# A windowed-attention, gated and mixer kernel: three loads moved ahead by a turn, and dummy matmuls in three waits

## The chip, the core and the metric

The kernel runs on one core of one Trainium2 chip. The metric is the device time of one execution in microseconds, less is better; it is given as the median of several runs. Its engines are TensorE (PE, with its weight loads PEld), VectorE (DVE), ScalarE (ACT), GpSimd (POOL) and SyncE (SP), which issues all of the DMAs here, in one queue.

## The reference

Three blocks follow each other: attention over a window of 64 keys, a gated block whose gate is mixed over the positions by `w_spatial`, and a token and channel mixer. Cut to what matters:

```python
# q, k, v: (4, 8, 576, 64)
scores = 0.125 * q @ k.T                       # only where 0 <= query - key < 64
attn = softmax(scores)
x = (attn @ v)  ->  (4, 576, 512)

h = relu(x @ w_in)                             # w_in: 512 x 1024
u, v = h[..., :512], h[..., 512:]
v_n = (v - mean(v)) / sqrt(var(v) + 1e-6)
v_s = einsum('ts,bsd->btd', w_spatial, v_n) + b_spatial      # w_spatial: 576 x 576
x = (u * v_s) @ w_out                          # w_out: 512 x 512

xt = x.transpose(0, 2, 1)                      # token mixer, then channel mixer
u = x + (relu(xt @ w_tok1) @ w_tok2).transpose(0, 2, 1)
out = u + relu(u @ w_ch1) @ w_ch2
```

The float64 weights are converted on the chip from their integer words; q, k, v and `w_spatial` are float32. Products of float32 accuracy are made of three matmuls, each operand being split into a high part (a cast on ScalarE) and a low part (a subtraction on VectorE).

## The kernel before, in words

The first part of the program (to some 220 us) is attention together with the gated block. Its order is written out by hand for every engine (`tc.manual_schedule`); each engine runs its instructions in that order. Behind it a scheduler orders the rest.

Attention goes over 18 iterations, `its`, each with up to 128 query rows of 8 heads. The loop over `n`, lines 517 to 553, is one *turn* each. Turn `n` does, for TensorE: the transposes of the normalised probabilities `pt(n)` (`att_turn`, line 283), one piece of the queued work (`run_work`), the products with v, `xo(n)` (`att_pv`, line 295), the scores of iteration `n + 2` (`scores`, lines 236 and 241), and then more queued work until a budget is used. ScalarE copies the transposes to SBUF (`PT(n)`, line 284), makes the exponentials of iteration `n + 1` (`sexp`, line 264), then converts `w_in` parts (L72, L441), casts `vf` (L355) and `xh(n)` (L309). VectorE normalises the exponentials (`snorm`, lines 272 to 274), writes `xl(n)` (L310), the maxima of the scores of iteration `n + 2` (`smax`, line 252 in the first iterations, line 255 from iteration 6 on) and other conversions.

The queued work consists of `uv_v` (12 matmuls per iteration: the v half of `x @ w_in`), `uv_u` (the u half, four groups of 12 matmuls every three iterations) and `spatial` (the product with `w_spatial`, from turn 7 on; its sums L392 and L393 run on VectorE and free the PSUM bank). Three PSUM banks (`psmm`) serve this work, four (`psa`, tag `sp`) the scores and transposes, and one (tag `xo`) the products with v. A bank is given to its next user when its last reader is done.

The loads: q and k of an iteration (`load_qk`, two buffers each) and v (`load_v`, two buffers each) are issued two turns ahead of their scores' or products' turn. `w_spatial` comes in ten parts, `ws_parts`; `load_ws(n)` at the end of a turn issues the next `n` parts into `raw` (three buffers) and has them cast to high (L101) and low parts (L103) in the same place of the order. `ws_at` says how many parts a turn takes. ScalarE's casts thus stand ahead of the next turn's copies PT. The first `w_out` loads (lines 569 and 570) use the same three buffers afterwards; they are ordered by the scheduler.

Before the loop, iterations 0 and 1 are scored and `w_in` is converted in parts. `keep_busy(k)` issues `k` matmuls of the identity, whose result nobody reads. Before, six of them stand before `pt(0)` and two before `pt(1)`.

Of the kernel before, what the change touches and what calls it, by code (L numbers as in the profile page):

```python
# [8 lines left out]
F32 = mybir.dt.float32  # L9
# [11 lines left out]
P = 128  # L21
# [14 lines left out]
def tile_kernel(ctx, tc, qT, kT, kE, v, w_in, wsT, b_sp, w_out, w_t1, w_t2, w_c1, w_c2, outT):  # L36

    nc = tc.nc

    def pool(name, side=None, stack=ctx, **kw):  # L40
        return stack.enter_context(tc.tile_pool(name=name, side=side, **kw))
# [4 lines left out]
    ident16 = const.tile([P, P], BF16, name="ident16")  # L46
# [58 lines left out]
    def load_split(*a, **kw):  # L105

        for _ in split_steps(*a, **kw):  # L110
            pass
# [55 lines left out]
    psmm = pool("psmm", bufs=3, space=PSUM)  # L167
# [7 lines left out]
    ws_h = ws[:, :5 * S].rearrange("p (k c) -> p k c", k=5)  # L175
    ws_l = ws[:, 5 * S:10 * S].rearrange("p (k c) -> p k c", k=5)
# [4 lines left out]
    att = pool("att", "right", stack=a_stack, bufs=2)  # L181
    psa = pool("psa", stack=a_stack, bufs=4, space=PSUM)

    def keep_busy(n):

        ps = psmm.tile([P, 512], F32, tag="mm", name="mm")
        for _ in range(n):
            nc.tensor.matmul(ps.rearrange("p (a c) -> p a c", a=4), ident16, ident16.unsqueeze(1).to_broadcast([P, 4, 128]), start=True, stop=True)

    its = [(p, i) for p in range(B // 2) for i in range(9)]  # L190
    held, vheld, soft, xt, vn = {}, {}, {}, {}, {}

    def where(p, i):

        return (2 * p + (i - 1) // 4, (i - 1) % 4) if i else (None, None)

    def load_qk(n):
        p, i = its[n]
        qq = att.tile([P, 4, 128], F32, tag="qq", name="qq")
        nc.sync.dma_start(out=qq.rearrange("p j t -> p (j t)"), in_=qT[n])  # L200
        kk = att.tile([P, 4, 256], F32, tag="kk", name="kk")
        if i:
            nc.sync.dma_start(out=kk.rearrange("p j k -> p (j k)")[:, :768], in_=kT[8 * p + i - 1])
            kk = kk.rearrange("p j k -> p (j k)")[:, :768].rearrange("p (j k) -> p j k", k=192)
        else:
            nc.sync.dma_start(out=kk.rearrange("p j k -> p (j k)"), in_=kE[p])
        held[n] = (qq, kk)

    def load_v(n):
        p, i = its[n]  # L210
        b, m = where(p, i)
        va = att.tile([P, 512], F32, tag="va", name="va")
        vb = att.tile([P, 512], F32, tag="vb", name="vb")
        if i:
            nc.sync.dma_start(out=va, in_=v[b, 128 * m:128 * m + 128, :])
            nc.sync.dma_start(out=vb, in_=v[b, 128 * m + 64:128 * m + 192, :])
        else:
            nc.sync.dma_start(out=va, in_=v[2 * p, S - 64:S + 64, :])
            nc.sync.dma_start(out=vb, in_=v[2 * p + 1, S - 64:S + 64, :])
        vheld[n] = (va, vb)  # L220
# [27 lines left out]
    def smax(n, g):  # L248
        scs, pb, nm, sm, mk = soft[n]
        if mk is None:  # L250
            mx = att.tile([P, 4], F32, tag="mx", name="mx", bufs=3)
            nc.vector.tensor_reduce(out=mx, in_=scs[g], op=ALU.max, axis=AX.X)
        else:
            for h in range(4):
                nc.vector.tensor_tensor_reduce(  # L255
                    out=pb[:, 4 * g + h, :], in0=scs[g][:, h, :], in1=mk, scale=-SCALE, scalar=3e38,
                    op0=ALU.add, op1=ALU.min, accum_out=nm[:, 4 * g + h:4 * g + h + 1])
            return
        nc.vector.tensor_scalar(out=nm[:, 4 * g:4 * g + 4], in0=mx, scalar1=-SCALE, scalar2=None, op0=ALU.mult)
# [13 lines left out]
        nc.vector.reciprocal(out=rs, in_=rs)  # L273
        nc.vector.tensor_tensor(out=pb[:, hs, :], in0=pb[:, hs, :], in1=rs.unsqueeze(2).to_broadcast([P, w, 128]), op=ALU.mult)  # L274

    def att_turn(n, banks=None):
        pb = soft.pop(n)[1]
        PT = att.tile([P, 8, 128], F32, tag="PT", name="PT", bufs=1)
        for g in range(2):
            pt = (banks.tile([P, 512], F32, tag="mm", name="pt").rearrange("p (h k) -> p h k", h=4) if banks  # L280
                  else psa.tile([P, 4, 128], F32, tag="sp", name="pt"))
            for h in range(4):
                nc.tensor.transpose(pt[:, h, :], pb[:, 4 * g + h, :], ident)  # L283
            nc.scalar.copy(out=PT[:, 4 * g:4 * g + 4, :], in_=pt)  # L284
        return PT

    def att_pv(n, PT, now=True):
        p, i = its[n]
        vt = vheld.pop(n)
        xo = psa.tile([P, 4, 128], F32, tag="xo", name="xo", bufs=1)  # L290
        for j in range(4):
            for q in range(2):
                for e in range(2):
                    hc = slice(64 * (2 * j + e), 64 * (2 * j + e) + 64)
                    nc.tensor.matmul(xo[64 * e:64 * e + 64, j, 64 * q:64 * q + 64], vt[q][:, hc],  # L295
                                     PT[:, 4 * e + j, 64 * q:64 * q + 64], start=True, stop=True)
        held[n] = xo
# [46 lines left out]
    def uv_v(p, i):  # L344

        xh, xl = xt[p, i // 3]
        ts_ = slice(128 * (i % 3), 128 * (i % 3) + 128)
        ps = psmm.tile([P, 512], F32, tag="mm", name="mm")
        mm3(ps, [(xh[:, k, ts_], xl[:, k, ts_], wi_h[:, k, 512:], wi_l[:, k, 512:]) for k in range(4)], late=(0, 1, 2) if p + i > 1 else (0, 2, 1))
        vv = lp.tile([P, 512], F32, tag="vf", name="vf", bufs=2)  # L350
        turns.append(normalise(p, i, ps, vv))
        tick()
# [21 lines left out]
    def tick():  # L374
        for t in list(turns):
            if next(t, turns) is turns:
                turns.remove(t)
# [36 lines left out]

    ws_parts = [(k, c) for k in range(5) for c in (0, 288)]

    def load_ws(n):
        for k, c in ws_parts[:n]:
            rows = P if k < 4 else 64
            load_split(ws_h[:, k, c:c + 288], ws_l[:, k, c:c + 288], wsT[128 * k:128 * k + rows, c:c + 288], rows=rows, dup=k == 4)  # L420
        del ws_parts[:n]

    def w_part(raw, src, hi, lo, cols):
# [29 lines left out]
    with tc.manual_schedule(engines={E.PE, E.SP, E.Activation, E.DVE, E.Pool}):  # L453
        wv = [wv_part(k) for k in range(4)]
        wu = [wu_part(ft) for ft in range(4)]

        def go(*ws):
            for w in ws:
                next(w, 0)

        load_qk(0)
        go(wv[0])
        load_qk(1)
        go(wv[1])
        load_v(0)
        go(wv[2])
        go(wv[3])
        go(wv[0])
        scores(0)
        smax(0, 0)  # L470
        smax(0, 1)
        go(wv[0])
        sexp(0, 0)
        go(wv[1])
        sexp(0, 1)
        go(wv[0])
        snorm(0, 0)
        snorm(0, 1)
        load_qk(2)
        load_v(1)  # L480
        go(wu[0])
        scores(1)
        keep_busy(6)
        PT = att_turn(0)
        smax(1, 0)
        smax(1, 1)
        go(wv[0])
        go(wv[1])
        go(wv[2])
        go(wv[1])  # L490
        go(wv[2])
        go(wv[3])
        att_pv(0, PT)
        go(wv[2])
        sexp(1, 0)
        go(wv[1])
        go(wv[3])
        go(wv[3])
        sexp(1, 1)
        go(wv[2])  # L500
        go(wv[3])
        load_v(2)
        load_qk(3)
        go(wu[1])
        go(wu[2])
        load_qk(4)
        go(wu[3])
        load_v(3)
        nc.sync.dma_start(out=bb, in_=bass.AP(b_sp.tensor, b_sp.offset, [[0, P], [1, S]]))
        scores(2)  # L510
        snorm(1)
        smax(2, 0)
        smax(2, 1)
        uv_v(*its[0])
        conv, late = {1: (0,), 2: (1, 2), 3: (3,)}, ()
        ws_at = {3: 2, 4: 3, 5: 3, 6: 2}
        for n in range(1, len(its)):
            more, some = n + 2 < len(its), n + 1 < len(its)
            cv = [wu[i] for i in conv.get(n, ())]
            if more and n > 1:  # L520
                if n > 2:
                    load_qk(n + 2)
                load_v(n + 2)
            if n == 1:
                keep_busy(2)
            PT = att_turn(n)
            go(*late)
            go(*late)
            go(*cv[:1])
            go(*cv[:1])  # L530
            if some:
                sexp(n + 1, 0)
                sexp(n + 1, 1)
                snorm(n + 1)
            go(*cv[:1])
            go(*cv[:1])
            tick()
            left = BUDGET - run_work(1)
            go(*cv[1:])
            att_pv(n, PT)  # L540
            go(*cv[1:])
            if more:
                scores(n + 2)
                smax(n + 2, 0)
                smax(n + 2, 1)
            if n > 1:
                tick()
            late = cv[1:]
            while work and left > 0:
                left -= run_work(1)  # L550
                tick()
            load_ws(ws_at.get(n, 0))
            enable(n)
        while turns:
            tick()
# [486 lines left out]
```

## Time and profile before

| | us |
|---|---|
| median of 3 runs (642.7, 644.18, 645.35) | 644.18 |
| the profiled execution | 642.67 |
| its span in the profile | 640.9 |
| TensorE busy in the span | 612.3 |
| VectorE busy | 461.9 |
| ScalarE busy | 333.4 |

The profile is of one execution. Its timeline gives for each group of instructions the start and the duration, and in brackets the idle time of the engine before it and what ended that; its windows give the busy time of engines in stretches of the span, with the clock that TensorE was granted (1.00 is 2.4 GHz, 0.50 is 1.2 GHz) and the share of time that DMA engines were busy. TensorE is busy for 96% of the span, the idle time lying mostly in the first 80 us, around 175 us and between 280 and 340 us.

### The profile page before, as it was taken

To read this page: it belongs to the slowest core of one execution; us is meant where nothing else is said; L and a number is where in the kernel's file an instruction comes from. 1 tells how busy PE (TensorE), PEld (TensorE's weight loads), DVE (VectorE), ACT (ScalarE), POOL (GpSimd) and SP (SyncE) were. 2 spreads that over 40 slices of the span, in tenths; PEclk is the share of its full clock that TensorE was granted. 3 is DMA by queue.
4 is the path that set the end of the run, shared out by engine and by line. 5 is a ranking of instruction groups with operands and counts; after the bars stand their busy time and mean duration, and the time that the engine had idled before them with its cause. 6 is when DMAs were issued, how large, how long until landed. Compare 5 with 4: busy or idle time off the path is not lost.

```text
span 640.9 us, 11957 instructions
## 1 busy us (share of the span) xinstructions
PE 612.3 (96%) x4440; PEld 570.2 (89%) x4440; DVE 461.9 (72%) x973; ACT 333.4 (52%) x835; POOL 151.9 (24%) x166
## 2 busy tenths in 40 slices
PE   6689799999999999999899999999999999999997
PEld 3468599899879999888798999999999999999987
DVE  4786757755575689678968973188976998867982
ACT  4677663444784264667544443355543646344550
POOL 6600000100000010556452582032000440002510
PEclk9889899999999999999999999999999999999999
DMA  8832653422240034557753719058434576534872
GB/s 324 279 98 97 200 167 96 146 76 75 76 156 27 2 107 145 181 200 237 292 191 118 263 74 337 1 170 281 139 134 132 201 229 211 164 115 139 269 241 75
DMA packets 46105, 103.60 MB, mean 162 GB/s; under 512 B 4192, under 2 KB 16736, under 8 KB 46048
## 3 DMA queue, kind: packets, MB, share of 16 engines
q1 hardware_dynamic: 46048, 102.84, 47.8%
q8 instruction: 35, 0.57, 0.4%
q14 instruction: 22, 0.18, 0.1%
HBM read 83.95 MB, written 18.87 MB: 160 GB/s over the span
## 4 chain that ended last, share of the span: by engine, by line
PE 67%; DVE 13%; ACT 7%; DMA 5%; issue 4%; POOL 2%; SPq 0%; DVEq 0%; ACTq 0%; POOLq 0%
PE mm L161 31%; PE A L894 17%; PE mm L823 7%; PE A L823 5%; ACT pb L264 3%; DMA scr<-hl 2%; PE pt L283 2%; PE xo L295 2%; DMA k<-in_w_c 2%; POOL k L728 1%; PE sc L241 1%; DVE ol L889 1%; DVE k L68 1%; DVE pb L274 1%; DVE k L69 1%
## 5 line engine op out<-in xcount | busy, mean ns | idle before, releaser
L894 PE MATMUL A<-oh,w 128*128 128x384 f32 x480 | 102.7, 334 | 0.0
L876 POOL TENSOR_TENSOR H<-H 128x384 f32<-128x384 f32 x36 | 44.8, 1258 | 182.6 <-DVE ol L889 171.2
L889 DVE TENSOR_TENSOR ol<-H,oh 128x384 fp32r<-128x384 f32 x120 | 79.8, 697 | 10.5 <-ACT oh L888 8.3
L894 PEld LDWEIGHTS A<-oh,w 128*128 128x128 f32 x480 | 85.0, 188 | 0.0
L888 ACT CAST oh<-H 128x384 fp32r<-128x384 f32 x120 | 59.8, 512 | 42.0 <-PE A L894 33.3
L894 PE MATMUL A<-ol,w 128*128 128x384 f32 x240 | 61.2, 336 | 2.2 <-DVE ol L889 2.2
L161 PE MATMUL mm<-ws,nh 128*128 128x288 f32 x320 | 61.9, 297 | 0.0
L161 PEld LDWEIGHTS mm<-ws,nh 128*128 128x128 f32 x320 | 49.9, 188 | 0.5 <-issue 0.3
L361 POOL TENSOR_SCALAR rstd<-mv 128x1 f32<-128x1 f32 x18 | 4.5, 249 | 184.1 <-DVE mv L360 183.9
L894 PEld LDWEIGHTS A<-ol,w 128*128 128x128 f32 x240 | 43.1, 188 | 3.2 <-DVE ol L889 3.1
L876 DVE TENSOR_TENSOR H<-H 128x384 f32<-128x384 f32 x36 | 23.6, 654 | 21.6 <-ACT H L816 19.3
L161 PE MATMUL mm<-ws,nl 128*128 128x288 f32 x128 | 37.7, 295 | 0.0
L264 ACT ACTIVATE pb<-pb,nm 128x128 f32<-128x128 f32 x96 | 37.2, 398 | 0.4 <-DVE nm L255 0.3
L272 DVE TENSOR_SCALAR rs<-sm 128x8 f32<-128x8 f32 (+1 forms) x19 | 3.2, 171 | 47.1 <-ACT pb L264 47.1
L284 ACT COPY PT<-pt 128x512 f32<-128x512 f32 x36 | 19.5, 591 | 30.8 <-PE pt L283 30.8
L161 PE MATMUL mm<-xh,wi_h 128*128 128x384 f32 x96 | 32.7, 341 | 0.7 <-ACT vf L355 0.6
L161 PE MATMUL mm<-xh,wi_l 128*128 128x384 f32 x96 | 32.1, 335 | 0.0
L161 PE MATMUL mm<-xl,wi_h 128*128 128x384 f32 x96 | 32.1, 334 | 0.0
L148 ACT CAST hl<-k 128x512 fp32r<-128x512 f32 (+1 forms) x24 | 13.6, 569 | 31.7 <-DVE k L69 16.3
L161 PE MATMUL mm<-gh,wo_l 128*128 128x512 f32 (+1 forms) x80 | 29.4, 370 | 0.0
L161 PE MATMUL mm<-gl,wo_h 128*128 128x512 f32 (+1 forms) x80 | 29.4, 370 | 0.0
L161 PE MATMUL mm<-gh,wo_h 128*128 128x512 f32 (+1 forms) x80 | 29.3, 376 | 0.0
(180 smaller groups left out, 1709.2 us busy)
## 6 DMA issues: line engine op xcount, KB each, us to landing
w<-scr SPq DMA_DIRECT2D x63, 512.0 KB, 4.3
k<-in_w_c SPq DMA_DIRECT2D x24, 512.0 KB, 5.5
scr<-hl SPq DMA_DIRECT2D x18, 512.0 KB, 5.1
kk<-in_kT SPq DMA_DIRECT2D x16, 384.0 KB, 4.9
k<-sums SPq DMA_DIRECT2D x12, 512.0 KB, 3.2
qq<-in_qT SPq DMA_DIRECT2D x18, 256.0 KB, 4.3
va<-in_v SPq DMA_DIRECT2D x18, 256.0 KB, 2.8
vb<-in_v SPq DMA_DIRECT2D x18, 256.0 KB, 3.1
```

Source lines behind the costliest of these rows:

```text
L68: nc.vector.scalar_tensor_tensor(out=y, in0=high, scalar=-0x80000000, in1=y, op0=ALU.bitwise_and, op1=ALU.bitwise_or)
L148: nc.scalar.copy(out=hi, in_=x)
L161: nc.tensor.matmul(o, a, c, start=(i == 0), stop=(i == n - 1))
L264: nc.scalar.activation(out=pb[:, h, :], in_=scs[g][:, h - 4 * g, :] if mk is None else pb[:, h, :], func=AF.Exp, scale=SCALE if mk is None ...
L283: nc.tensor.transpose(pt[:, h, :], pb[:, 4 * g + h, :], ident)
L284: nc.scalar.copy(out=PT[:, 4 * g:4 * g + 4, :], in_=pt)
L295: nc.tensor.matmul(xo[64 * e:64 * e + 64, j, 64 * q:64 * q + 64], vt[q][:, hc], PT[:, 4 * e + j, 64 * q:64 * q + 64], start=True, stop=True)
L823: nc.tensor.matmul(o, a, m, start=first and i == 0, stop=i == len(todo) - 1, skip_group_check=True)
L876: eng.tensor_tensor(out=out, in0=a, in1=b, op=ALU.subtract)
L888: nc.scalar.copy(out=oh, in_=blk[j])
L889: nc.vector.tensor_tensor(out=ol, in0=blk[j], in1=f(oh), op=ALU.subtract)
L894: nc.tensor.matmul(acc[d], a, m, start=(first and j == 0 and i == 0), stop=(last and j == NJ - 1 and i == 2), skip_group_check=True)
```

## The change

- q and k of iteration `n + 3` are loaded at the start of turn `n`, instead of those of `n + 2`; v stays at `n + 2`.
- `load_ws` first completes the casts of the parts that its last call issued, then issues its own, without casting them. `ws_at` begins one turn earlier (turns 2 to 5 instead of 3 to 6, with the same numbers of parts).
- Seven dummy matmuls, written to the bank `xo`, stand before `uv_v(0)`. The two before `pt(1)` now write to the bank that the transposes use afterwards, and eight such stand before `pt(2)`.

```diff
-    def keep_busy(n):
-
-        ps = psmm.tile([P, 512], F32, tag="mm", name="mm")
+    def keep_busy(n, ps=None):
+
+        ps = ps or psmm.tile([P, 512], F32, tag="mm", name="mm")
...
-    def att_turn(n, banks=None):
+    def att_turn(n, banks=None, busy=0):
...
+            for _ in range(0 if g else busy):
+                nc.tensor.matmul(pt, ident16, ident16.unsqueeze(1).to_broadcast([P, 4, 128]), start=True, stop=True)
...
+    ws_open = []
+
     def load_ws(n):
+
+        for t in ws_open:
+            for _ in t:
+                pass
+        ws_open.clear()
         for k, c in ws_parts[:n]:
             rows = P if k < 4 else 64
-            load_split(ws_h[:, k, c:c + 288], ws_l[:, k, c:c + 288], wsT[128 * k:128 * k + rows, c:c + 288], rows=rows, dup=k == 4)
+            ws_open.append(split_steps(ws_h[:, k, c:c + 288], ws_l[:, k, c:c + 288], wsT[128 * k:128 * k + rows, c:c + 288], rows=rows, dup=k == 4))
+            next(ws_open[-1])
...
+        keep_busy(7, psa.tile([P, 512], F32, tag="xo", name="xo", bufs=1))
         uv_v(*its[0])
...
-        ws_at = {3: 2, 4: 3, 5: 3, 6: 2}
+        ws_at = {2: 2, 3: 2, 4: 3, 5: 3}
...
-            if more and n > 1:
-                if n > 2:
-                    load_qk(n + 2)
-                load_v(n + 2)
-            if n == 1:
-                keep_busy(2)
-            PT = att_turn(n)
+            if n > 1:
+                if n + 3 < len(its):
+                    load_qk(n + 3)
+                if more:
+                    load_v(n + 2)
+            PT = att_turn(n, busy={1: 2, 2: 8}.get(n, 0))
```

How this moves instructions, at three places. SP in turns 4 and 5 (`qq` and `kk` are q and k, `va` and `vb` v, `raw` the buffers of the spatial weights), before:

```order
L215 DMA va<-in_v 128x512
L216 DMA vb<-in_v 128x512
L85 DMA raw<-in_wsT 128x288 x3
L200 DMA qq<-in_qT 128x512
L203 DMA kk<-in_kT 128x768
```

The same place on SP in the changed program, with the end of turn 3 ahead of it:

```order
L85 DMA raw<-in_wsT 128x288 x2
L200 DMA qq<-in_qT 128x512
L203 DMA kk<-in_kT 128x768
L215 DMA va<-in_v 128x512
L216 DMA vb<-in_v 128x512
L85 DMA raw<-in_wsT 128x288 x3
```

The parts that are cast at the end of turn 4 are now the two at the top of this piece; the three at its foot are those that turn 5 casts. In the piece from before, the three `raw` loads are cast in turn 4 itself.

ScalarE from the end of turn 3 into turn 5 (`ws` are the spatial weights, `PT` the copied transposes, `pb` the exponentials), before:

```order
L101 CAST ws<-raw 128x288 x2
L284 COPY PT<-pt 128x512 x2
L264 ACTIVATE pb,sm<-sc,nm 128x128 x8
L355 ACTIVATE vf<-mm 128x512
L309 CAST xh<-xo 128x4x128
L101 CAST ws<-raw 128x288 x3
```

And in the changed program:

```order
L101 CAST ws<-raw 128x288 x2
L286 COPY PT<-pt 128x512 x2
L264 ACTIVATE pb,sm<-sc,nm 128x128 x8
L357 ACTIVATE vf<-mm 128x512
L311 CAST xh<-xo 128x4x128
L101 CAST ws<-raw 128x288 x2
```

The casts stand in the same places; at the end of turn 4 there is one less, and at the end of turn 6, further down, three instead of two.

TensorE between `uv_v(0)` and the transposes of turn 1 (`mm` and `pt` are PSUM banks, `ident` the identity), before:

```order
L161 MATMUL mm<-wi_l,xh 128x512 x4
L188 LDWEIGHTS ident_63
L188 MATMUL mm<-ident_63 128x512
L188 LDWEIGHTS ident_63
L188 MATMUL mm<-ident_63 128x512
L283 MATMUL pt<-ident,pb 128x128 x8
```

And in the changed program:

```order
L161 MATMUL mm<-wi_l,xh 128x512 x4
L283 LDWEIGHTS ident_63
L283 MATMUL pt<-ident_63 128x512
L283 LDWEIGHTS ident_63
L283 MATMUL pt<-ident_63 128x512
L285 MATMUL pt<-ident,pb 128x128 x8
```

The two dummies stay where they were but write to `pt`. The seven stand in front of the first row of `uv_v(0)`, and eight more pairs like these stand in front of the transposes of turn 2. From turn 3 on TensorE's order is the same in both programs.

## Rows read from the trace of the kernel before

**Rows 1.** Windows, one stretch: us, busy time (and count) of each engine, clock, DMA.

```profile
80.00:96.00 16.00, 16.00 (x177) 15.57 (x178) 8.35 (x31) 10.41 (x42) 0.79 (x2) 1.00 0.51 166
```

**Rows 2.** Timeline of TensorE, turns 0 to 2: start, us, line, tile, count, [idle before].

```profile
22.34 0.51 PE L161 MATMUL mm<-wi_h,xh 128*128 128x512 f32 x1 [0.93 <-ACT wi_h L441]
...
25.81 0.91 PE L188 MATMUL mm<-ident 128*128 128x512 bf16 x2
...
26.56 1.04 PE L283 MATMUL pt<-ident,pb 128*128 128x128 f32 x8
...
33.54 1.94 PE L283 MATMUL pt<-ident,pb 128*128 128x128 f32 x8 [2.44 <-DVE pb L274]
```

**Rows 3.** Windows of 1 us, TensorE alone: us, busy time, granted clock, DMA share, GB/s.

```profile
25.00:26.00 1.00, 1.00 (x4) 0.50 1.05 412
...
75.00:76.00 1.00, 1.00 (x6) 0.50 0.92 270
```

**Rows 4.** Timeline of VectorE and ScalarE, turns 0 to 2.

```profile
19.05 0.69 DVE L310 TENSOR_TENSOR xl<-xo,xh 128x512 fp32r<-128x512 f32 x1 [0.36 <-ACT xh L309]
...
24.17 1.22 DVE L274 TENSOR_TENSOR pb<-pb,rs 128x1024 f32<-128x1024 f32 x1
...
27.25 1.07 ACT L284 COPY PT<-pt 128x512 f32<-128x512 f32 x2 [0.61 <-PE pt L283]
...
36.00 0.64 ACT L72 ACTIVATE mm<-U 128x512 f32<-128x512 f32 x1
...
36.57 0.35 ACT L264 ACTIVATE pb<-sc,nm 128x128 f32<-128x128 f32 x1
```

**Rows 5.** Timeline of TensorE, turn 4.

```profile
58.06 1.04 PE L283 MATMUL pt<-ident,pb 128*128 128x128 f32 x8
58.85 1.18 PE L161 MATMUL mm<-wi_h,xh 128*128 128x512 f32 x4
...
61.80 0.34 PE L295 MATMUL xo<-PT,va 128*64 128x64 f32 x4
...
62.88 1.10 PE L241 MATMUL sc<-kk,qq 64*64 64x128 f32 x32
```

**Rows 6.** Timeline of ScalarE and VectorE, end of turn 4 and turn 5.

```profile
63.61 0.66 ACT L309 CAST xh<-xo 128x512 fp32r<-128x512 f32 x1
66.48 0.80 ACT L101 CAST ws<-raw 128x288 fp32r<-128x288 f32 x2 [2.20 <-DMA raw<-in_wsT]
...
68.91 1.06 ACT L284 COPY PT<-pt 128x512 f32<-128x512 f32 x2
69.87 0.41 ACT L264 ACTIVATE pb<-pb,nm 128x128 f32<-128x128 f32 x1
...
66.32 0.28 DVE L255 CUSTOM_DVE_ANT_0 pb<-sc,msk 128x128 f32<-128x128 f32 x1
```

**Rows 7.** Timeline of TensorE, starts of turns 5 and 6, first `uv_u` of turn 6.

```profile
65.16 1.06 PE L283 MATMUL pt<-ident,pb 128*128 128x128 f32 x8 [1.18 <-DVE pb L274]
...
74.90 1.94 PE L283 MATMUL pt<-ident,pb 128*128 128x128 f32 x8 [2.69 <-DVE pb L274]
...
82.07 0.44 PE L161 MATMUL mm<-xh,wi_h 128*128 128x384 f32 x1
```

**Rows 8.** The tile `raw`, 40 to 100 us: time from issue to landing.

```profile
DMA to landing us min/median/max: 2.6/3.3/3.8
```

**Rows 9.** Timeline of VectorE, turn 7: last subtractions, first spatial sum.

```profile
92.04 0.83 DVE L103 TENSOR_TENSOR ws<-raw,ws 128x288 fp32r<-128x288 f32 x2
...
98.08 0.45 DVE L392 TENSOR_TENSOR tmp<-mm,bb 128x288 f32<-128x288 f32 x1
```

**Rows 10.** Chain of the work that ended last: start, us, what.

```profile
3.05 7.55 DMA U<-in_w_in
...
97.36 7.78 PE mm L161 x56
```

**Rows 11.** DMA issues, 40 to 100 us: count, KB each, median us to landing.

```profile
raw<-in_w_out SPq DMA_DIRECT2D x5, 256.0 KB, 3.5
```

## The prediction, made before the change was run

> **What bounds the kernel now.** I read the windows by stretch first. From 80 to 96 us TensorE is busy for the whole window at the full clock [rows 1]; the idle time further down, around 175 us and from 280 us on, lies where the change leaves the order of work as it is, apart from a few loads of `w_out`. What it can win or lose therefore lies in the first 80 us, and whatever it wins there moves all later work forward. In that first part I then read TensorE's timeline together with those of ScalarE and VectorE. Three things cost time.
>
> First, turns 0 to 2. TensorE waits for short chains on ScalarE and VectorE, and after such waits its matmuls run at half speed: nine matmuls of `uv_v(0)` go from 22.34 to 25.81, and the transposes `pt(2)` take 1.94 us after an idle time of 2.44 [rows 2]. The granted clock in 25 to 26 us is 0.50, the 1.2 GHz level [rows 3]. Second, at the end of turn 4 ScalarE stands in front of the casts of the spatial weights (L101) until their loads land, and the copies of the transposes, PT(5), stand behind these casts [rows 6]. Third, that delay reaches TensorE as an idle time of 2.69 us before `pt(6)` at 74.90 [rows 7], and turn 6 starts at the 1.2 GHz level again [rows 3].
>
> **Dummies, part one: seven before `uv_v(0)`, two before `pt(1)`.** The seven write the bank of `xo(0)`, so the first waits until VectorE has read it: xl(0) ends at 19.05 + 0.69 = 19.74 [rows 4]. One matmul of 512 columns takes (61.80 - 58.85) / 12 = 0.25 us at full clock [rows 5], so seven end at 21.5. The first three matmuls of `uv_v(0)` then end at 22.2, before the fourth, which starts at 22.34 and waits for a cast, not for TensorE. So at full clock the dummies cost nothing. They fill most of the idle time between the scores and `uv_v(0)`, and I take it that the clock stays up; then nine matmuls take 9 x 0.25 = 2.2 us and end at 24.55 instead of 25.81. The two dummies behind them only change place and bank; they end at 25.05. `pt(1)` needs the normalised pb(1), written until 24.17 + 1.22 = 25.39 [rows 4]. With 0.15 us for the handover it starts at 25.55 instead of 26.56 [rows 2]: **1.0 us**, no more, since VectorE is next.
>
> **Dummies, part two: eight before `pt(2)`.** PT(1), the exponentials of turn 2 and its normalisation all hang on `pt(1)`, so `pt(2)` moves from 33.54 to 32.5. The scores of turn 3 end where TensorE's 2.44 us of idle time begin, at 33.54 - 2.44 = 31.1, now 30.1. Eight dummies take 2.0 us and end at 32.1, before pb(2) is there: no cost, by 0.4 us. With the clock up, `pt(2)` and its copies take as long as in turn 1, where the copies start 0.69 after the transposes and end 1.76 after them (26.56; 27.25 + 1.07) [rows 2, 4], so PT(2) ends at 34.3. ScalarE then runs L72 and reaches the exponentials 0.57 later (36.00 to 36.57), at 34.85 [rows 4]. VectorE's maxima for them follow the normalisation directly and move with `pt(2)`; before, they were done shortly ahead of the exponentials, now they arrive together with ScalarE. The exponentials move from 36.57 to 34.85, that is **1.7 us** for both parts, of which the second brings 0.7. From there to the first `uv_u` of turn 3 VectorE is occupied almost without a gap, and I carry the 1.7 through it unchanged.
>
> **Loads of the spatial weights a turn ahead.** In turn 4 the casts are now two instead of three, and their data were issued in turn 3. ScalarE ends xh(4) at 63.61 + 0.66 = 64.27; two casts take 0.80, to 65.07 [rows 6]. The copies need the transposes, 65.16 + 0.69 = 65.85 [rows 4, 7]. So PT(5) starts at 65.85 instead of 68.91, and the exponentials of turn 6 at 66.81 instead of 69.87 [rows 6]: **3.1 us**. VectorE writes the maxima from 66.32 on [rows 6], just in time. Then normalisation and `pt(6)` follow at 71.84 instead of 74.90. TensorE is ready before that: `uv_v` ends at about 68.9, the outputs and scores take 2.2 more, 71.1. So VectorE's normalisation is next in line, and 0.7 us of idle time are left where there were 2.69.
>
> Does the clock hold over this 0.7? TensorE had 1.18 idle before `pt(5)` [rows 7] and ran on at full speed. So I take full clock for turn 6: from `pt` to the first `uv_u` it took 82.07 - 74.90 = 7.17 [rows 7]; the same work in turn 4 took 62.88 + 1.10 - 58.06 = 5.92 [rows 5]. That is 1.25, rounded **1.3 us**.
>
> Each load has to arrive. The second load of turn 3 reuses the buffer of a part cast at the end of that turn, so SP waits there; by the ends above it is issued some 5 us before its cast, and these loads land within 3.8 us [rows 8]. In turn 4 two of three loads wait for that turn's subtractions, about 69 us, and land near 72.5; the casts of turn 5 then end near 73 and PT(6) near 74, while TensorE asks for it only at 75.6 after `uv_v`. Covered by 1.5 us. Behind the waiting SP stand q and k of three turns ahead and v of two, none of which is needed within 8 us.
>
> **q and k three turns ahead: nothing.** Before, no matmul in turns 3 to 12 waits for them; they land earlier and compete with loads that have time. It costs up to the 0.5 us that a delayed cast might take out of the 1.5 of cover, so nothing in the sum.
>
> **The sum.** 1.7 + 3.1 + 1.3 = 6.1 us. The profiled execution took 642.67 (span 640.9 and 1.77 around it), which gives 636.6; the median of three is 644.18, 1.51 higher, and I forecast against it: **638.1 us**. The bounds of the parts: dummies from -0.9 (if the clock is down when they start, eight take 512 columns / 1.2 GHz = 0.43 each, 3.4 in all, and push `pt(2)` from 32.5 to 33.5, while seven push `uv_v(0)` behind its cast) to 1.7 and another 1.5, if the runs above the profiled one are long because their clock falls oftener. The loads from 2.2 to 3.1, the clock of turn 6 from 0 to 1.3.
>
> The Trainium skill (TensorE: Matmul & The Clock Gate, Part 1) says that the point at which the clock changes shifts from run to run of one kernel. The three runs here, 2.65 us apart, would agree with that but don't show that it is the clock. By it the clock terms of one profile are one draw of several.
>
> **Rivals.** (a) *The dummies buy nothing.* The clock falls anyway, or VectorE absorbs what turn 1 wins. For it: VectorE is the next bound everywhere in turns 1 to 3. Against: ScalarE waits over 2 us for the slow transposes of `pt(2)`. Then 3.1 + 1.3 remain, 639.8; without the clock of turn 6 also 641.1.
>
> (b) *The casts still wait.* The buffers, three of them, are refilled only after the subtractions, so a load "a turn ahead" may be issued late. If the casts of turn 4 wait as long as the last one did before, only the dummies' 1.7 and some of the rest are left: 641 to 642.5.
>
> (c) *The output weights block VectorE: slower.* The first w_out loads now queue on SP behind the last spatial weights; they wait for the subtractions at 92.04 to 92.9 [rows 9] and their first conversion stands on VectorE before turn 7's spatial sums (L392), which give TensorE its PSUM buffers back. TensorE needs the first at 97.36 + 7.78 / 4 = 99.3 [rows 10], when the first of four groups ends; before, the sum was done at 98.08 + 0.45 [rows 9]. Counting back over normalisation and conversion, the load has to land by about 96.9. Issued at 92.5 with the median landing of 3.5 [rows 11] it is there at 96.0. With the longest wait for a load in this trace, 7.55 [rows 10], it lands at 100.1 and TensorE stops for 3.2: 641.3. Slower than before by over 0.5% only from a landing of some 14 us. The Trainium skill (DMA: Bandwidth & Descriptors, Latency and other measured facts) gives 0.2 us of memory latency on average and 2 us at high load; by it alone the landing would grow by 1.8, a stop of under 1 us and about 639. No run here shows that.
>
> **How the numbers follow.** Faster or slower "by over 0.5%" means 3.2 us, about what a measurement of this kernel can tell from no change. Forecast, 635 to 640: 0.67. Rival (a): 0.18, two thirds of it faster by over 0.5%. Rival (b): 0.08, a quarter of it. Rival (c): 0.07, half of it slower or near, since other late collisions of moved loads belong here too. Faster: 0.64 + 0.12 + 0.02 = 0.78 less 0.02 for the edge at 641, so 0.76; slower 0.04; the rest 0.20. The range takes the forecast's low end and reaches over (a) to the middle of (b): 635.0 to 641.5.
>
> **What would show it.** Right: seven dummies from about 19.7, granted clock 1.00 throughout 23 to 37 us, `pt(2)` near 32.5 and about 1 us long, no ScalarE wait for the spatial weights at the end of turn 4, `pt(6)` at 74.90 - 4.8 = 70.1 and about 1 us long, first `uv_u` of turn 6 at 76.0. Wrong: a half-clock stretch in the first 80 us, casts that still wait in turn 4, or an idle TensorE behind VectorE in turn 7.

## The result, and the profile after

The changed kernel takes 638.37 us (median of 6 runs, 636.93 to 639.03), the kernel before beside it 643.44 (6 runs, 642.13 to 645.35). The ratio is 0.9918, with a 95% interval from 0.9899 to 0.9937: faster by 5.1 us. The forecast was 638.1. It is nearer to the measured time than its sum is to the measured gain: 6.1 us had been taken off a median of 644.18, and more runs of the kernel before put that median 0.74 lower. That two errors of the same sign cancel in the time is luck.

The profiled execution took 636.93 us, its span is 5.7 us shorter. The page of the changed kernel (span; busy time, share and count of TensorE; its granted clock in 40 slices, in tenths):

```profile
span 635.2 us, 11997 instructions
...
PE 610.3 (96%) x4455; PEld 567.5 (89%) x4455; DVE 461.6 (73%) x973; ACT 332.9 (52%) x835; POOL 152.3 (24%) x166
...
PEclk9999999999999999999999999999999999999999
```

TensorE is busy for 2.0 us less, although it runs 15 more dummies: fewer of its matmuls run at half speed. The windows of two stretches (us; busy time and count of each engine; clock; DMA share; GB/s) answer to [rows 3]:

```profile
23.00:26.00 3.00, 2.46 (x15) 1.39 (x13) 2.90 (x6) 1.15 (x3) 2.17 (x1) 1.00 1.04 383
...
74.00:78.00 4.00, 4.00 (x68) 3.76 (x63) 3.22 (x8) 3.00 (x12) 0.00 (x0) 1.00 0.33 88
```

In [rows 3] a window of each of these stretches stood at 0.50. TensorE's timeline of the changed kernel, answering to [rows 2] and [rows 7]:

```profile
19.04 1.67 PE L188 MATMUL xo<-ident 128*128 128x512 bf16 x7 [1.80 <-DVE xl L312]
...
21.59 0.50 PE L161 MATMUL mm<-wi_h,xh 128*128 128x512 f32 x1 [0.19 <-ACT wi_h L451]
...
24.70 1.09 PE L285 MATMUL pt<-ident,pb 128*128 128x128 f32 x8 [0.33 <-DVE pb L274]
...
29.22 1.90 PE L283 MATMUL pt<-ident 128*128 128x512 bf16 x8
31.64 1.09 PE L285 MATMUL pt<-ident,pb 128*128 128x128 f32 x8 [0.52 <-DVE pb L274]
...
69.70 1.06 PE L285 MATMUL pt<-ident,pb 128*128 128x128 f32 x8 [0.78 <-ACT ws L101]
...
75.56 0.44 PE L161 MATMUL mm<-xh,wi_h 128*128 128x384 f32 x1
```

All transposes here take about 1.1 us, where two of them took 1.94. The wait before `pt(2)` is 0.52 us instead of 2.44, because dummies lie in it, and the one before `pt(6)` 0.78 instead of 2.69. ScalarE and VectorE of the changed kernel, end of turn 4 into turn 5 (answering to [rows 6]):

```profile
61.88 0.87 ACT L101 CAST ws<-raw 128x288 fp32r<-128x288 f32 x2
63.70 1.07 ACT L286 COPY PT<-pt 128x512 f32<-128x512 f32 x2 [0.94 <-PE pt L285]
...
68.33 1.23 DVE L274 TENSOR_TENSOR pb<-pb,rs 128x1024 f32<-128x1024 f32 x1
```

The two casts no longer wait for a load; now ScalarE waits 0.94 us for the transposes. L274 ends at 69.56 and `pt(6)` starts 0.14 later, the handover that other transposes have after it; the bracket names the cast only because it ended a little later.

**A common start for comparing.** The start of an execution varies: the fourth matmul of `uv_v(0)` waits for a cast of a `w_in` part that arrives between 21.6 and 23.6 us in these profiles, whatever the kernel. So I count from that matmul. Starts of the transposes from there, in us:

| kernel | `pt(1)` | `pt(2)` | `pt(3)` | `pt(4)` | `pt(5)` | `pt(6)` |
|---|---|---|---|---|---|---|
| before (22.34) | 4.22 | 11.20 | 19.09 | 35.72 | 42.82 | 52.56 |
| changed (21.59) | 3.11 | 10.05 | 17.50 | 34.28 | 41.39 | 48.11 |
| changed, once more (22.53) | 3.11 | 10.35 | 17.53 | 34.30 | 41.40 | 48.13 |
| loads, no new dummies (23.40) | 4.87 | 12.21 | 20.23 | 36.58 | 43.69 | 50.41 |
| dummies alone (22.71) | 3.11 | 10.07 | 17.53 | 34.29 | 41.40 | 51.28 |
| without the seven (23.62) | 4.20 | 11.09 | 18.28 | 35.04 | 42.16 | 48.88 |
| without the eight (23.59) | 3.11 | 10.17 | 17.54 | 34.30 | 41.41 | 48.14 |
| the same, second execution (23.39) | 3.12 | 10.16 | 18.14 | 34.30 | 41.41 | 48.13 |

The steps are separate in it: from the kernel before to the changed one, 1.44 us are won up to `pt(4)`, nothing between `pt(4)` and `pt(5)`, 3.02 between `pt(5)` and `pt(6)` (9.74 became 6.72), and from `pt(6)` to the first `uv_u` 7.17 became 5.86, another 1.31. These are 5.77. The execution also began 0.75 earlier, which the change did not do.

**What was given back.** At `pt(8)` and at `pt(9)` 5.32 of the 5.77 are left; the difference lies in turn 7. VectorE and TensorE there, answering to [rows 9]:

```profile
91.47 0.45 DVE L394 TENSOR_TENSOR tmp<-mm,bb 128x288 f32<-128x288 f32 x1
91.84 0.28 DVE L63 TENSOR_SCALAR val<-val 128x256 int32<-128x256 int32 x1
...
96.43 0.45 DVE L394 TENSOR_TENSOR tmp<-mm,bb 128x288 f32<-128x288 f32 x1
...
96.94 0.54 PE L161 MATMUL mm<-ws,nh 128*128 128x288 f32 x2 [0.34 <-DVE tmp L394]
```

From the first spatial sum to the third it takes 4.96 us; before, 4.42 (98.08 to 102.50). Two more conversions of `w_out` (L63 and L68, 0.5 together) now stand between them, and TensorE waits 0.34 us for a bank. Since 5.7 = 0.75 + 5.32 - 0.38, another 0.38 is lost behind `pt(9)`. It is lost at one place in the part that the scheduler orders, where TensorE waits for a copy on ScalarE, before and after:

```profile
308.36 0.40 PE L161 MATMUL mm<-t_h,hh 128*128 128x288 f32 x1 [1.00 <-ACT U L638]
```

```profile
302.74 0.40 PE L161 MATMUL mm<-t_h,hh 128*128 128x288 f32 x1 [1.46 <-ACT U L648]
```

ScalarE stands there behind a cast of another weight (L148) that waits for VectorE's conversion, and this cast starts at 300.61 instead of 306.21, 5.6 earlier, where TensorE had come 6.1 earlier. Of the 5.7, then, some 4.9 come from the change, which fits the difference of the medians, 5.1.

### The profile page after: what moved, and what is told of

Same layout as the page of the kernel before. It is cut to its first block, busy times and chain, and to the rows that moved or that the text cites. A ratio compares the mean times of both kernels' runs of the same rounds, so it can differ in the third digit from the quotient of the medians.

```text
span 635.2 us, 11997 instructions
## 1 busy us (share of the span) xinstructions
PE 610.3 (96%) x4455; PEld 567.5 (89%) x4455; DVE 461.6 (73%) x973; ACT 332.9 (52%) x835; POOL 152.3 (24%) x166
## 4 chain that ended last, share of the span: by engine, by line
PE 65%; DVE 14%; ACT 7%; issue 5%; DMA 4%; POOL 3%; SPq 1%; DVEq 0%; POOLq 0%; ACTq 0%
PE mm L161 29%; PE A L904 17%; PE mm L833 7%; PE A L833 5%; ACT pb L264 3%; PE xo L297 2%; PE pt L285 2%; DMA scr<-hl 2%; DVE k L68 1%; POOL k L738 1%; DVE k L69 1%; PE sc L241 1%; DVE ol L899 1%; DMA U<-in_w_in 1%; DVE k L63 1%
## 5 line engine op out<-in xcount | busy, mean ns | idle before, releaser
L886 DVE TENSOR_TENSOR H<-H 128x384 f32<-128x384 f32 x36 | 23.6, 654 | 21.6 <-ACT H L826 19.3
L148 ACT CAST hl<-k 128x512 fp32r<-128x512 f32 (+1 forms) x24 | 13.7, 570 | 32.5 <-DVE k L69 15.8
```

Source lines behind the costliest of these rows:

```text
L148: nc.scalar.copy(out=hi, in_=x)
L886: eng.tensor_tensor(out=out, in0=a, in1=b, op=ALU.subtract)
```

## The experiments

Three theories were to be told apart: the gain is mostly the loads' (3.1 + 1.3), with the dummies' 1.7 on top; or the dummies buy nothing, rival (a); and, for the part that I had put at nothing, that q and k three turns ahead do carry something.

**The loads without the new dummies.**

```diff
-        keep_busy(7, psa.tile([P, 512], F32, tag="xo", name="xo", bufs=1))
         uv_v(*its[0])
...
-            PT = att_turn(n, busy={1: 2, 2: 8}.get(n, 0))
+            if n == 1:
+                keep_busy(2)
+            PT = att_turn(n)
```

> The change without its dummies (the two old ones back in their place). My theory: the loads bring 3.1 us in turn 5 and 1.3 by the clock of turn 6, less 0.4 in turn 7, so about 4.0 faster than before (ratio 0.9938); uv_v(0) and pt(2) run partly at the 1.2 GHz level as before, pt(6) starts about 3 us earlier relative to pt(5) and is 1.1 us long. Rival: the dummies carry the whole gain, since the wait for the loads was covered by other work anyway; then this is within 0.5 us of before.

Measured: 639.84 us (12 runs) against 643.44 (29 runs), ratio 0.9943 (0.9926 to 0.996). The granted clock from 23 to 26 us is 0.50 again, `pt(2)` takes 1.77 us, and from `pt(5)` to `pt(6)` it takes 6.72 us, as in the changed kernel. The loads carry 3.6 us alone. This interval overlaps that of the changed kernel (0.9899 to 0.9937), so that the times by themselves do not show that the dummies add anything to the loads.

**The dummies without the loads.**

```diff
+        keep_busy(7, psa.tile([P, 512], F32, tag="xo", name="xo", bufs=1))
         uv_v(*its[0])
...
-            if n == 1:
-                keep_busy(2)
-            PT = att_turn(n)
+            PT = att_turn(n, busy={1: 2, 2: 8}.get(n, 0))
```

> The kernel before with the 17 dummies alone. My theory: 1.5 us faster than before (ratio 0.9977): full clock from 20 to 37 us, pt(2) 1.1 us long, the ScalarE wait for the spatial weights at the end of turn 4 and the 2.7 us of idle time before pt(6) still there, and turn 6 at the 1.2 GHz level. Rival: VectorE absorbs what the clock gives back, 0 to 0.3 us. Other rival: the dummies delay TensorE, slower by up to 1.5 us.

Measured: 642.55 us (12 runs), ratio 0.9984 (0.9966 to 1.0002); the interval reaches from 2.2 us won to nothing. In its profile the dummies do all that they do in the changed kernel (34.29 to `pt(4)`), and then it is lost: ScalarE's wait for the spatial weights and TensorE's wait before `pt(6)` are still there, and this time the half clock behind that wait lasts longer. Timeline of ScalarE and TensorE, then windows of the same stretch:

```profile
66.14 0.84 ACT L101 CAST ws<-raw 128x288 fp32r<-128x288 f32 x2 [2.91 <-DMA raw<-in_wsT]
...
73.99 1.94 PE L285 MATMUL pt<-ident,pb 128*128 128x128 f32 x8 [2.69 <-DVE pb L274]
```

```profile
74.00:78.00 4.00, 4.00 (x14) 3.52 (x15) 3.96 (x22) 2.00 (x5) 0.79 (x2) 0.50 0.79 235
78.00:82.00 4.00, 4.00 (x52) 3.09 (x54) 1.70 (x6) 4.00 (x19) 0.00 (x0) 0.74 0.01 3
```

In the kernel before, the stretch from 78 us on was at 1.00; here it is at 0.74. From `pt(6)` to the scores behind it, 7.68 us pass instead of 6.14. Whether half clocks are this long in every run with the dummies alone, one profile can't tell; the profiled execution, 643.96, is one of the longer of the 12 (640.06 to 644.42).

**q and k three turns ahead alone, and the loads' turn ahead without it.** The first takes only the change of `load_qk` from `n + 2` to `n + 3`; the second only that of `load_ws` and `ws_at`:

```diff
-        ws_at = {3: 2, 4: 3, 5: 3, 6: 2}
+        ws_at = {2: 2, 3: 2, 4: 3, 5: 3}
```

> The kernel before with q and k loaded three turns ahead and nothing else. My theory: no difference (within 0.3 us), since no matmul of turns 3 to 12 waits for them. Rival: the loads of the spatial weights land earlier, because 0.6 MB of q and k no longer stand behind them in the same burst; then the wait before pt(6) shrinks and 1 to 3 us are won by this part alone.

> The kernel before with the spatial weights' loads a turn ahead of their casts and nothing else (q and k two turns ahead, no new dummies). My theory: all of the loads' gain, about 4.0 us faster than before, like loads_only. Rival: q and k two turns ahead now stand on SP behind loads that wait for buffers and come late to the scores, so that part of the gain is lost, 1 to 3 us.

Measured: q and k alone 644.28 us (12 runs), ratio 1.0009 (0.999 to 1.0028), no change. The loads' turn ahead without them **656.08 us** (5 runs), ratio 1.0192 (1.0162 to 1.0223): 12.6 us slower than before, and 16.2 slower than the same loads with q and k three turns ahead. SyncE's timeline of this kernel, turns 3 to 5 (its "duration" contains the time that it waits for a buffer), then TensorE's, and, of the waits of SyncE from 40 to 95 us, those for the buffers of the spatial weights (total, times, longest):

```profile
50.75 14.37 SPq L85 DMA_DIRECT2D raw<-in_wsT  x2
...
65.65 0.42 SPq L203 DMA_DIRECT2D kk<-in_kT  x1
...
69.40 1.10 PE L241 MATMUL sc<-kk,qq 64*64 64x128 f32 x32 [1.38 <-DMA kk<-in_kT]
...
79.41 1.99 PE L241 MATMUL sc<-kk,qq 64*64 64x128 f32 x32 [4.05 <-DMA kk<-in_kT]
...
91.29 1.98 PE L241 MATMUL sc<-kk,qq 64*64 64x128 f32 x32 [4.41 <-DMA kk<-in_kT]
```

```profile
SPq L85 <- DVE ws L103: 25.9, 4, 13.6
```

At the end of turn 3 SyncE stands 14.37 us in front of a buffer that is free only when that turn's casts and their subtractions (L103) are done, and q and k of the scores of turn 4 stand behind it: k is issued at 65.65 and lands near 69.4, and TensorE waits for it there. TensorE waits four times so, for 13.1 us in all (3.26 in turn 3, and the three shown). The scores behind the longer waits take 1.98 us instead of 1.10, so the waits cost more than their length. In the changed kernel SyncE waits in the same place:

```profile
47.14 10.73 SPq L85 DMA_DIRECT2D raw<-in_wsT  x2
57.92 0.43 SPq L200 DMA_DIRECT2D qq<-in_qT  x1
```

The q and k behind it, however, are those that the scores of turn 5 need. The Trainium skill (DMA: Bandwidth & Descriptors, Anatomy of one DMA — SWDGE (gpsimd) path) says, in a section on DMAs that GpSimd issues, that any wait for a semaphore happens on the issuing sequencer before the transfer is dispatched; for the DMAs of SyncE the rows here agree, the 14.37 us standing on SyncE and holding up q and k, which stand behind.

**Is it the queue, or the loads?** Here the cause of one of SyncE's waits is taken away: the end of turn 3 issues a single part, which finds a free buffer, and casts none. q and k stay two turns ahead, and there are no new dummies; the rest of the loads is that of the spread casts, further down.

```diff
-        ws_at = {3: 2, 4: 3, 5: 3, 6: 2}
+        ws_at = {2: 2, 3: 1, 4: 3, 5: 3}
...
-            load_ws(ws_at.get(n, 0))
+            load_ws(ws_at.get(n, 0), n != 3)
```

> The kernel before with q and k two turns ahead, no new dummies, and the loads of spread_casts: in turn 3 only one part is issued, into a buffer that is free. My theory: in ws_only SP stood for 14 us before the second part of turn 3, with q and k of turn 4's scores behind it; here the wait of these scores for kk (1.4 us) is gone, while the waits in turns 5 and 6 (4.1 and 4.4 us) stay, since there SP still waits for buffers. Rival: kk comes late for another reason, such as the sum of the loads in flight; then all three waits stay.

Measured: 655.92 us (one execution). SyncE and TensorE, then the same line of SyncE's waits from 40 to 95 us:

```profile
50.90 0.33 SPq L85 DMA_DIRECT2D raw<-in_wsT  x1
...
51.75 0.42 SPq L203 DMA_DIRECT2D kk<-in_kT  x1
...
79.85 1.92 PE L241 MATMUL sc<-kk,qq 64*64 64x128 f32 x32 [4.99 <-DMA kk<-in_kT]
...
90.68 1.98 PE L241 MATMUL sc<-kk,qq 64*64 64x128 f32 x32 [3.24 <-DMA kk<-in_kT]
```

```profile
SPq L85 <- DVE ws L103: 12.6, 4, 7.5
```

Where SyncE has no buffer to wait for, k goes out at 51.75 and the scores of turn 4 don't wait; where it still has, in turns 5 and 6, they wait as in the kernel above. TensorE's wait follows the queue. (SyncE also stands 16.2 us in front of a load of v here, but q and k of turn 4 have been issued ahead of it.) A third wait, of 3.31 us in turn 3, comes behind a load of turn 2 that stands 4.58 us on SyncE; it is in both kernels, and I had not listed it. TensorE's waits for k are 11.5 us in all, 1.6 less, yet the time is the same within 0.2; where the 1.6 went I did not follow. A version with more buffers, which would take the waits away altogether, was not run.

**Which of the dummies?** Two kernels leave out the seven or the eight:

```diff
-        keep_busy(7, psa.tile([P, 512], F32, tag="xo", name="xo", bufs=1))
```

> The changed kernel without the seven dummies before uv_v(0). My theory: the clock falls during uv_v(0) as before, pt(1) is up to 1 us later relative to the fourth matmul of uv_v(0), and the kernel takes 0.5 to 1.0 us longer than the changed one (ratio to before 0.993). Rival: VectorE's normalisation sets pt(1) anyway and nothing is lost (ratio 0.9918).

```diff
-            PT = att_turn(n, busy={1: 2, 2: 8}.get(n, 0))
+            PT = att_turn(n, busy={1: 2}.get(n, 0))
```

> The changed kernel without the eight dummies before pt(2). My theory: TensorE idles 2.4 us before pt(2), the clock then falls, pt(2) is about 1.9 us long again, and 0.5 to 0.7 us are lost against the changed kernel (ratio to before 0.9927). Rival: with the seven in place the clock is still up after the idle time and pt(2) stays 1.1 us long; nothing is lost.

Measured against 644.31 (13 runs): without the seven 639.15 (6 runs), ratio 0.9928 (0.9903 to 0.9954); without the eight 639.16 (6 runs), 0.993 (0.9908 to 0.9953); the changed kernel, run again beside them as a yardstick:

> The changed kernel once more, beside the others on the same chip. Both theories: 0.9918 of before, within 0.2%.

638.47 (6 runs), 0.9921 (0.9897 to 0.9944). The times don't separate the three; the profiles do. Without the seven, `pt(1)` is 1.1 late and `pt(4)` 0.76. The eight by themselves do carry something: from `pt(1)` to `pt(4)` this kernel takes 30.84 us, where the three profiles without any new dummies (before, the loads, q and k alone) take 31.50 to 31.71. Without the eight, TensorE is idle for 2.46 us before `pt(2)`, but the clock stayed at 1.00 and nothing was late at `pt(3)`. The clock might have been luck, so this kernel was run twice more:

> The changed kernel without the eight dummies, a second profile. If the seven alone keep the clock up, pt(2) is again 1.1 us long and the granted clock 1.00 from 30 to 37 us. If that depends on the execution, it is about 1.9 us long this time or in the third profile, and turn 3 starts 0.5 us later relative to pt(1).

> The same kernel, a third profile, with the same two expectations.

Measured: 639.47 and 638.6 us (one execution each). Windows of the first execution of this kernel from 33 to 36 us, and of the second from 33 to 36 and 36 to 40 us:

```profile
33.00:36.00 3.00, 2.25 (x14) 1.86 (x15) 2.82 (x5) 1.53 (x3) 1.20 (x3) 1.00 0.78 254
```

```profile
33.00:36.00 3.00, 2.46 (x12) 2.20 (x13) 2.78 (x6) 1.61 (x3) 1.07 (x2) 0.75 0.82 250
36.00:40.00 4.00, 4.00 (x42) 3.01 (x42) 3.02 (x8) 3.83 (x18) 0.00 (x0) 0.76 0.08 31
```

TensorE's timeline in the second:

```profile
33.55 1.06 PE L285 MATMUL pt<-ident,pb 128*128 128x128 f32 x8 [2.45 <-DVE pb L274]
34.37 1.93 PE L161 MATMUL mm<-wi_h,xh 128*128 128x512 f32 x4
```

In the second execution the clock did fall after the same idle time, but only behind `pt(2)`, which took 1.06 us in all three; in the third it didn't fall. Where it fell, `pt(3)` came 0.6 later, but `pt(4)` was at 34.30 as ever, so that other engines than TensorE set the end of that turn. So with the seven in place, the eight guard against a fall that costs nothing by turn 4.

**Two versions that go on.** The two casts at the end of turn 3 stand ahead of the exponentials that `pt(5)` needs, and TensorE waits 1.22 us before `pt(5)`. Late casts: the first parts are issued a turn later, so that nothing is cast at the end of turn 3, and the last two parts are issued in the middle of turn 6.

```diff
-        ws_at = {2: 2, 3: 2, 4: 3, 5: 3}
+        ws_at = {3: 2, 4: 3, 5: 3}
...
+            if n == 6:
+                load_ws(2)
```

> The changed kernel with no casts of spatial weights at the end of turn 3: two, three and three parts are issued at the ends of turns 3, 4 and 5 and cast at the ends of turns 4 and 5 and in the middle of turn 6, where the last two are issued, to be cast at its end. My theory: the two casts (0.8 us) that stand ahead of PT(4) set pt(5), so pt(5) and all after it come 0.8 us earlier than in the changed kernel (ratio to before 0.9905). Rival: the casts of turn 4 now wait for loads issued only a few us before, or SP is held up, and nothing is won or up to 3 us are lost.

Measured: 640.11 us (8 runs), ratio 0.9939 (0.9918 to 0.9959). From `pt(4)` to `pt(5)` it takes 6.44 instead of 7.11, as expected, but TensorE pays 1.37 us in turns 6 and 7, where the last parts come late:

```profile
81.52 0.44 PE L161 MATMUL mm<-xh,wi_h 128*128 128x384 f32 x1 [0.19 <-ACT vf L357]
...
89.14 0.40 PE L161 MATMUL mm<-ws,nh 128*128 128x288 f32 x1 [0.72 <-ACT ws L101]
90.00 0.68 PE L161 MATMUL mm<-ws,nh 128*128 128x288 f32 x3 [0.46 <-DVE ws L103]
```

Spread casts: no cast at the end of turn 3, one part fewer there, and the last one issued after the second `uv_u` group of turn 6.

```diff
-        ws_at = {2: 2, 3: 2, 4: 3, 5: 3}
+        ws_at = {2: 2, 3: 1, 4: 3, 5: 3}
...
+                done += 1
+                if n == 6 and done == 2:
+                    load_ws(1)
-            load_ws(ws_at.get(n, 0))
+            load_ws(ws_at.get(n, 0), n != 3)
```

> The changed kernel with the casts spread otherwise: two parts issued in turn 2 and one in turn 3, all three cast at the end of turn 4, three more at the end of turn 5, three behind the second uv_u of turn 6 and the last at its end. My theory: PT(4) and with it pt(5) come 0.8 us earlier, the third cast of turn 4 costs up to 0.3 of it, no cast waits for a load and turn 7 waits for no cast; 0.5 us faster than the changed kernel (ratio to before 0.991). Rival: the casts among the uv_u of turn 6 wait for their loads and hold up the PSUM banks, as in late_casts; 0.5 to 1.4 us lost.

Measured: 638.95 us (9 runs) against 643.09 (14 runs), ratio 0.9936 (0.9916 to 0.9957). The 0.66 are won again (6.45), and lost in turn 7. ScalarE, VectorE and TensorE:

```profile
86.72 0.43 ACT L101 CAST ws<-raw 128x288 fp32r<-128x288 f32 x1 [1.23 <-DMA raw<-in_wsT]
...
97.87 0.42 DVE L69 SCALAR_TENSOR_TENSOR val<-raw,val 128x256 int32<-128x256 int32 x1
98.21 0.45 DVE L394 TENSOR_TENSOR tmp<-mm,bb 128x288 f32<-128x288 f32 x1
...
98.71 0.53 PE L161 MATMUL mm<-ws,nh 128*128 128x288 f32 x2 [1.32 <-DVE tmp L394]
```

ScalarE waits 1.23 us for the last part, so its exponentials and VectorE's normalisation come 0.7 us later against TensorE's spatial products than in the changed kernel, and one more conversion (L69) has moved ahead of the third sum, 0.34. Together that is the 1.0 by which TensorE's wait has grown (1.32 instead of 0.34). Neither version beats the changed kernel.

## Why the prediction was right, point by point

- **Dummies before `uv_v(0)`: 1.0 us, right** (1.11 at `pt(1)`). The seven end before the cast that `uv_v(0)` waits for, the clock stays up, and VectorE's normalisation is next, as said. The seven took 1.67 us where 7 x 0.25 had given 1.75.
- **Dummies before `pt(2)`: another 0.7 us, wrong; nothing beside the seven.** The exponentials of turn 3 came 1.48 earlier, not 1.7, and without the eight they are as early. The step that failed is the addition: the second part was to come from a `pt(2)` at full clock, but behind the seven `pt(2)` runs at full clock without the eight too (1.06 us in three executions of three). Where the seven are absent, the eight bring the 0.7 that was forecast. ScalarE's first exponential of turn 3 in the changed kernel, without the eight (second execution) and without the seven, from the fourth matmul of `uv_v(0)` 12.75, 12.78 and 13.53 (before 14.23):

```profile
34.34 0.37 ACT L264 ACTIVATE pb<-sc,nm 128x128 f32<-128x128 f32 x1 [0.35 <-DVE nm L259]
```

```profile
36.17 0.37 ACT L264 ACTIVATE pb<-sc,nm 128x128 f32<-128x128 f32 x1 [0.29 <-DVE nm L259]
```

```profile
37.15 0.37 ACT L264 ACTIVATE pb<-sc,nm 128x128 f32<-128x128 f32 x1
```

  With the seven ScalarE waits for VectorE's maxima, so copies of `pt(2)` that came still earlier would not have helped. And the maxima do not "follow the normalisation directly and move with `pt(2)`": `wi_l`, `vf` (L366) and `xl` stand between, and `vf` waits for GpSimd. Timelines of GpSimd and VectorE in the changed kernel:

```profile
28.73 1.96 POOL L440 TENSOR_SCALAR sign<-U 128x512 int32<-128x512 int32 x1 [0.33 <-DVE mm L448]
30.77 0.91 POOL L363 TENSOR_SCALAR rstd<-mv 128x1 f32<-128x1 f32 x1
...
32.36 0.55 DVE L366 TENSOR_SCALAR vf<-vf,mv,rstd 128x512 f32<-128x512 f32 x1 [0.18 <-POOL rstd L364]
...
33.43 0.68 DVE L252 TENSOR_REDUCE mx<-sc 128x4 f32<-128x512 f32 x1
```

  GpSimd's sign of a `w_in` part (L440) stands ahead of `rstd`. The wait is 0.18 us, most of what the 1.48 lacks of 1.7. I had followed three engines and not the fourth.
- **Loads a turn ahead: 3.1 us, right** (3.02), with the casts' wait gone, the copies behind the transposes and VectorE next in line, 0.78 us idle where 0.7 was forecast. `pt(6)` came at 69.70 (forecast 70.1), but 0.75 of that is the earlier start; counted from the fourth matmul it came 4.45 earlier, where 4.8 had been forecast.
- **Clock of turn 6: 1.3 us, right** (1.31).
- **q and k three turns ahead: nothing, right alone and wrong as a part of the change.** Alone it measures nothing. But it is what lets the loads move at all: without it they cost 16.2 us more. I had read that SyncE waits and that what stands behind it isn't needed within 8 us; this holds only because q and k are a turn further ahead. The step had been costed against the program before, where the long waits of SyncE from 40 to 95 us (38.7 us in all, until products with v are done) stand in front of v's loads, behind that turn's q and k, and not against the program with the other step in it.
- **Rival (c), the output weights on VectorE in turn 7.** The place was right, the size small: 0.34 us instead of up to 3.2. The loads did not come late; their conversions stand between the sums.
- **Rival (a), dummies that buy nothing,** is not refused by the times, whose intervals overlap. For the seven it is refused by the profiles up to turn 4: the eight profiles with them reach `pt(4)` at 34.27 to 34.64, the four without them in which no scores wait (before, the loads, q and k alone, without the seven) at 35.04 to 36.58. For the eight it holds beside the seven, not by themselves.
- **The sum.** 5.77 of 6.1 arrive at the first `uv_u` of turn 6, and some 4.9 at the end. What the forecast lacked was a term for what the later order gives back, 0.8 us.
- **The chances.** In the sum for "faster" 0.64 stands for the forecast, to which 0.67 had been given; the 0.03 are not accounted for.

## What to carry to other kernels

Where a queue issues all loads in order, a load that waits for its buffer holds up every load behind it: before moving one ahead, list what stands behind it in the new order and when that is needed, and cost the steps of a change together, since a step that is worth nothing alone can be what another stands on. A dummy matmul is worth its place only where the next engine in line has time to use what it wins; here filling either of two waits won time up to turn 4, and filling both no more than the first. Two gains that both come from a clock that stays up can't be added without asking what the first leaves to the second. Follow all engines to the next wait, GpSimd too.

## What the runs showed of the hardware

- The same idle time does not always lower the clock. After 2.45 us of idle in the kernel without the eight it fell in one of three executions (0.75 from 33 to 36 us, 1.00 in the other two); in the kernel with the dummies alone the half clock after 2.69 us reached further than before. The Trainium skill (TensorE: Matmul & The Clock Gate, Part 1) says that the transition to full clock shifts from run to run; these profiles show the like of the fall.
- The clock in the windows reads 1.00 from the start, where durations do not fit it. In TensorE's timeline of the changed kernel, the same 32 matmuls of the scores:

```profile
5.27 1.98 PE L241 MATMUL sc<-kk,qq 64*64 64x128 f32 x32 [0.54 <-DMA kk<-in_kE]
...
16.13 1.10 PE L241 MATMUL sc<-kk,qq 64*64 64x128 f32 x32
```

  The first group takes almost twice the time, while the window from 3 to 7 us states 1.00. Half clock would fit the 1.98 us; no row shows it. So early in a span the windows' clock is not enough, and the durations have to be read beside it.
